# Two more blocks of a layer's second product in Strassen's form, with attention paced closer and its transposed blocks moved inside SBUF

## The chip, the cores and the metric

The kernel runs on one core of a Trainium2 chip. The metric is device time in microseconds (us) of one execution, as the median of several runs. One execution was also profiled; the rows below are of that one, and times in them count from the start of its span. The engines are TensorE (PE, with PEld for its weight loads), VectorE (DVE), ScalarE (ACT), GpSimd (POOL) and SyncE (SP), which issues nearly all DMAs.

## The reference

Inputs are float64 from NumPy, except the attention inputs (float32). What is computed, cut to what matters:

```python
# attention: batch 4, 8 heads, 768 tokens, head_dim 64, 8 memory keys; chunks of 32 tokens
q_c = q[:, :, c_start:c_end]                      # 32 tokens
k_full = concatenate([mem_k, k[:, :, l_start:r_end]])   # 16 to the left, 8 to the right
a = softmax(scale * q_c @ k_full.T); out[c] = a @ v_full
x = out as 3072 tokens x 512
# layer one, then layer two; w_in 512 x 2048, w_out 2048 x 512
h = x @ w_in;  x = maximum(0.01 * h, h) @ w_out
h = x @ w_in2; y = (h * clip(h + 3, 0, 6) / 6) @ w_out2
```

## The kernel before

**Tiling.** The 3072 tokens are six blocks of 512. Every large matmul is 128x128 by 128x512, and each product is taken three times, since operands are split in a high and a low part (`wh xh + wh xl + wl xh`). In the plain ("classical") form a block of layer one is sixteen steps f; a step is `hidden` (12 matmuls into one `ph` bank), the activation (`act_1` and `act_3` on ACT, `act_4` on DVE, which leave the split `g` in SBUF), and `output` (12 matmuls into four `py` banks that add up over f). `output` of step f-1 stands behind `hidden` of step f on TensorE. After f=15 `done` empties the four banks and `stored` writes them to `y_dram`.

In Strassen's form two blocks go together: `h_product` and `o_product` do 7 products where the plain form does 8, so 336 matmuls for each of the two products of a pair (plain: 384). The x of a pair is mixed into seven operands (`mix` L1035, `high` L1039 on ACT, `low` L1043 on DVE), as are the weights: quarters of a pair of weight tiles are summed (`c_first`, `c_more`), stored to `w_dram` (`c_store` L1007), loaded in units of 512 KB (`cw_load` L1010) and split (`cw_high` L1014, `cw_low` L1018). The activated hidden values are stored to `g_dram` (`g_store` L1089) and loaded again as operands of `o_product` (`g_load` L1092).

Before, blocks one to four of layer one are plain, blocks five and six are a Strassen pair, and all of layer two is three Strassen pairs (all hidden stages, then all output stages).

**What runs beside it.** In block one the weights of layer one arrive as float64 and are turned into float32 parts, one unit of two tiles per step: `w_load` L303, `w_upper` L313 and `w_lower` L319 on ACT, `w_clip` L323, `w_shift` L327, `w_join` L334, `w_add` L341 on DVE, `w_high` L345 on ACT, `w_low` L350 on DVE. The temporary of units 13, 14 and 15 lies in a ring `wa` of one buffer, that of the others in a ring `raw` of two. From block two on, `combine_first` (16 times) adds the parts of layer one's weights up again (`c_whole` L964), sums quarters and stores all seven; `combine` (16 times) converts a pair of tiles of layer two's weights and does the same.

Attention of tokens 1024 on goes in sixteen double visits of TensorE, `PACE` apart in the plan: scores of two pairs of chunks (L441) and the values of an earlier double visit (L617). Between them, in one buffer `both`: `a_masked_two` L475 and `a_most_two` L494 on DVE, eight exponentials L498 on ACT, `a_sums` L572 on POOL, `a_inverse` L576 on DVE, `a_norm_two` L509 (two on POOL) and a 32x32 block transpose `a_turn` L584 on DVE; then `turn_store` L587 to DRAM and three `turn_load` L590 to the layout that the values matmul reads. The values of a double visit are taken two visits after its scores.

**Order.** A planner in the kernel simulates engines, rings of buffers and a DMA pipe with the durations in `TIME`, picks at each moment the ready step with the earliest due time, and the program is written out in that order. Each engine and each DMA queue then runs its own list in order: a step that is late holds up what stands behind it. The due times of the stages come from `block_at`, `hidden_at` and `output_at`.

Of the kernel before, what the change touches and what calls it, by code (L numbers as in the profile page):

```python
# [22 lines left out]
    words=(0.67, 1.14), clip=(0.41, 0.69), shift=(0.42, 0.7), join=(0.68, 1.22), add=(0.78, 1.22), high=(0.62, 1.05), low=(0.68, 1.22), load=0.47,  # L23
# [8 lines left out]
LANDING, RATE = 2.1, 290e3  # L32
# [6 lines left out]
ORDER = (16, 18, 20, 22, 32, 34, 24, 26, 28, 30, 36, 38, 40, 42, 44, 46)  # L39
# [8 lines left out]
CLASSICAL = 4  # L48
LATEST = 0.0
W0 = 9  # L50
W1 = 0
W2 = 0
W3 = 1
W4 = 3
PACE = 17.0
LAST_STEP = 12.0
SPREAD = 3.0
# [4 lines left out]
DEEP = 1  # L62

# [125 lines left out]
def tile_kernel(  # L189
# [35 lines left out]
    CTX = LC + PT + RC  # L225
# [15 lines left out]
    turn_dram = [dr.tile([P, W // 32, 2 * HP * 32], F32, tag=f"td{j}", name=f"turn_dram{j}") for j in range(2)]  # L241
# [6 lines left out]
        [dr.tile([P, n, NF // 2, TB], F32, tag=f"gd{y}{c}", name=f"g_dram{y}{c}") for c in range(4)]  # L248
        for y, n in enumerate([(NB - CB) // 2, NB // 2])
# [8 lines left out]
    qk_t = at.tile([P, HP * (PT + W)], F32, tag="qk", name="qk_now")  # L258
    v_t = at.tile([W, HD], F32, tag="v", name="v_now")
# [92 lines left out]
    w_ready = {}  # L352

    def convert(wanted):

        for f in [0, NF, *range(1, NF)]:
# [14 lines left out]
            c = add("DVE", T["add"][n], u - 2.4, w_add, key, after=[c, l], frees=raw)  # L371
            c = add("ACT", T["high"][n], u - 1.6, w_high, key, after=[c, loaded[NPB - 1], w_ready.get((0, 0, 0))], takes=w)
# [13 lines left out]
    def inputs(pr):  # L386
        n = HP * (PT + W)
        if pr >= NPB:
            t, vt = qk_t, v_t
            if doubled(pr) and pr % 2:  # L390
                t, vt = in_t[pr][0][:, :n], in_t[pr][-1][:W, :HD]
# [8 lines left out]
    def raw_buffer(pr, j):  # L400
        in_t.setdefault(pr, []).append(raw_pair(1).rearrange("p a c -> p (a c)")[:, j * HP * (PT + W):])

    def load_qk(pr):
        if doubled(pr) and pr % 2:
            raw_buffer(pr, 0)
        nc.sync.dma_start(out=inputs(pr)[0], in_=qk[divmod(pr, PPB)])

    def load_v(pr):
        if doubled(pr) and pr % 2:
            raw_buffer(pr, 1)  # L410
        assert pr in in_t or pr >= NPB
        nc.sync.dma_start(out=inputs(pr)[3], in_=v[divmod(pr, PPB)])
# [34 lines left out]
    def a_masked(pr):  # L447
# [12 lines left out]
        for n in range(2):  # L460
            if p == 0:
                nc.vector.memset(e[n * PT:n * PT + CH, :, 0:LC], NEG)
            if p == PPB - 1:
                nc.vector.memset(e[n * PT + CH:(n + 1) * PT, :, CTX - RC:CTX], NEG)
# [7 lines left out]
    def a_masked_two(pr):  # L472
# [10 lines left out]
        for k in range(2):  # L483
            p = (pr + k) % PPB
            for n in range(2):
                if p == 0:
                    nc.vector.memset(e[n * PT:n * PT + CH, k, :, 0:LC], NEG)
                if p == PPB - 1:
                    nc.vector.memset(e[n * PT + CH:(n + 1) * PT, k, :, CTX - RC:CTX], NEG)
# [122 lines left out]
    def a_values(pr, pt, at=0, every=PT):  # L612
        t, vt = aT_t.pop(pr), inputs(pr)[3]
# [27 lines left out]
    def x_store(pr):  # L641
        at = (pr - 1) * PT - CB * TB
        nc.sync.dma_start(out=x_dram[:, :, at:at + 2 * PT], in_=out_t.pop(pr))
# [10 lines left out]
    def finish(pr, c, t, p):  # L654

        blk = pr // NPB
        if blk >= CB:
            y = [("ye", ("xs", pr))]
            c = add("ACT", T["copy"], t + 0.8, x_staged, pr, after=[c], takes=y, frees=p)
            d = add("SP", T["load"], t + 1.5, x_store, pr, after=[c], frees=y, nbytes=P * 2048)  # L660
# [30 lines left out]
    def visit_two(d, q, t):  # L691

        after, takes, frees, more, p = [], [], [], {}, None
        if d < NP:
            scores_in[d] = d
            a = add("SP", T["load"], t - 17, load_qk, d, after=loaded[-1:], takes=[("qk", d)], nbytes=P * 640 * 4)
            b = add("SP", T["load"], t - 17, load_qk, d + 1, after=[a, *scored[-1:]], nbytes=P * 640 * 4,
                    takes=[("raw", 1)] if d == 2 * NPB else [])
            loaded.extend([a, b])
            after += [a, b]  # L700
# [892 lines left out]
```

## Time and profile before

| what | value |
|---|---|
| median of 3 runs | 1051.37 us (1050.51 to 1052.44) |
| the profiled execution, its own time | 1051.67 us |
| its span, first to last instruction | 1049.9 us |
| granted TensorE clock, mean over the span | 1.000 |
| PE / DVE / ACT / POOL busy | 1037.9 / 809.0 / 612.1 / 151.2 us |
| DMA | 222.34 MB, 212 GB/s over the span |

Busy time is the time in which an engine had an instruction running. The own time is 1.8 us longer than the span, which is what lies around it. Matmuls overlap in the pipeline, so a matmul of 390 ns in a row does not cost 390 ns: rows of a chain with a count tell what one costs.

### The profile page before, as it was taken

What the parts mean: (1) busy time and instruction counts of PE and PEld (TensorE: products, weight loads), DVE (VectorE), ACT (ScalarE), POOL (GpSimd) and SP (SyncE); (2) the same over time, 40 slices, a digit from 0 to 9 for tenths busy, and PEclk for the clock granted to TensorE, in tenths of its full rate; (3) what the DMA queues carried; (4) which work ended last, traced back from release to release, by engine and by line L of the source; (5) the groups of instructions that cost most, each with busy time, mean ns of one, the idle gap of its engine ahead of it and who ended that gap; (6) DMA issues with size and microseconds to landing.
All of it is one profiled execution on the core that took longest, in us unless ns stands there. A gap on an engine that the chain in (4) does not pass through costs nothing. (4 is left out here: it accounts for less than half of the span.)

```text
span 1049.9 us, 16361 instructions
## 1 busy us (share of the span) xinstructions
PE 1037.9 (99%) x6023; PEld 851.7 (81%) x6023; DVE 809.0 (77%) x1096; ACT 612.1 (58%) x1115; POOL 151.2 (14%) x153
## 2 busy tenths in 40 slices
PE   9999999999999999999999999999999999999997
PEld 8777788888888888888888888888888888888886
DVE  6999877657676666867799997978747896686784
ACT  7886754444545555677567666657667544444451
POOL 4122111101111110012100021120365400000000
PEclk9999999999999999999999999999999999999999
DMA  9664477778777899588966865664667557257213
GB/s 291 205 210 144 155 271 240 223 240 264 235 235 249 299 273 279 184 298 286 356 223 204 266 217 186 212 233 147 227 216 255 203 150 212 51 162 193 60 56 61
DMA packets 150081, 222.34 MB, mean 212 GB/s; under 512 B 35312, under 2 KB 90608, under 8 KB 150000
## 3 DMA queue, kind: packets, MB, share of 16 engines
q1 hardware_dynamic: 148912, 221.03, 65.8%
q8 instruction: 47, 0.77, 0.3%
q10 hardware_dynamic: 1088, 0.26, 0.1%
q14 instruction: 34, 0.28, 0.1%
HBM read 137.36 MB, written 83.89 MB: 211 GB/s over the span
## 5 line engine op out<-in xcount | busy, mean ns | idle before, releaser
L836 PE MATMUL py<-g,w 128*128 128x512 f32 x768 | 188.6, 392 | 0.0
L836 PE MATMUL ph<-xh,w 128*128 128x512 f32 x512 | 171.0, 393 | 0.0
L836 PEld LDWEIGHTS py<-g,w 128*128 128x128 f32 x768 | 142.7, 188 | 29.9
L836 PEld LDWEIGHTS ph<-xh,w 128*128 128x128 f32 x512 | 95.9, 188 | 21.3 <-DVE w L350 0.8
L836 PE MATMUL ph<-xl,w 128*128 128x512 f32 x256 | 99.9, 390 | 0.6 <-DVE xl L649 0.6
L1086 POOL TENSOR_TENSOR gated<-gated,gated 128x512 f32<-128x512 f32 x32 | 51.3, 1619 | 320.0 <-DVE gated L1083 211.7
L854 ACT ACTIVATE ph<-ph 128x512 f32<-128x512 f32 x64 | 37.3, 583 | 82.4 <-PE ph L836 81.0
L1046 PE MATMUL sB<-x,cw 128*128 128x512 f32 x336 | 80.9, 389 | 0.0
L1046 PEld LDWEIGHTS sB<-x,cw 128*128 128x128 f32 x336 | 63.1, 188 | 13.1
L863 DVE TENSOR_TENSOR g<-ph,g 128x512 fp32r<-128x512 f32 x64 | 43.9, 686 | 30.9 <-ACT g L858 30.4
L1014 ACT CAST cw<-cw 128x1024 fp32r<-128x1024 f32 x56 | 58.9, 1051 | 13.4 <-DMA cw<-w_dram 13.1
L1046 PE MATMUL sE<-xwa,cw 128*128 128x512 f32 x276 | 66.4, 389 | 0.0
L1046 PE MATMUL sE<-fb,cw 128*128 128x512 f32 x264 | 63.5, 389 | 0.0
L1046 PEld LDWEIGHTS sE<-xwa,cw 128*128 128x128 f32 x276 | 51.7, 188 | 10.9 <-DVE xwa L1043 0.2
L498 ACT ACTIVATE raw<-raw,mx 128x96 f32<-128x96 f32 x128 | 46.4, 366 | 20.1 <-DVE mx L494 20.1
L1046 PEld LDWEIGHTS sE<-fb,cw 128*128 128x128 f32 x264 | 49.5, 188 | 10.5 <-DVE fb L1043 0.2
L1018 DVE TENSOR_TENSOR cw<-cw 128x1024 fp32r<-128x1024 f32 x42 | 51.6, 1235 | 6.4 <-ACT cw L1014 6.4
L836 PEld LDWEIGHTS ph<-xl,w 128*128 128x128 f32 x256 | 48.1, 188 | 10.4 <-DVE xl L649 0.9
L572 POOL TENSOR_SCALAR su<-su 128x4 f32<-128x4 f32 (+1 forms) x32 | 11.5, 360 | 265.4 <-ACT raw L498 216.4
L1046 PE MATMUL sD<-x,cw 128*128 128x512 f32 x204 | 49.3, 389 | 0.0
L1046 PE MATMUL sA<-fb,cw 128*128 128x512 f32 x204 | 49.0, 389 | 0.0
L1046 PE MATMUL sB<-xwb,cw 128*128 128x512 f32 x204 | 49.0, 389 | 0.0
(170 smaller groups left out, 2174.0 us busy)
## 6 DMA issues: line engine op xcount, KB each, us to landing
g_dram<-gated SPq DMA_DIRECT2D x128, 256.0 KB, 3.2
cw<-w_dram SPq DMA_DIRECT2D x56, 512.0 KB, 5.6
raw<-g_dram SPq DMA_DIRECT2D x32, 512.0 KB, 4.3
f<-in_moe_w_dram SPq DMA_DIRECT2D x15, 1024.0 KB, 5.0
cv<-in_moe_w_in_dram SPq DMA_DIRECT2D x8, 1024.0 KB, 6.7
w_dram<-raw SPq DMA_DIRECT2D x32, 256.0 KB, 4.3
w_dram<-cv SPq DMA_DIRECT2D x32, 256.0 KB, 2.8
cv<-in_moe_w_out_dram SPq DMA_DIRECT2D x8, 1024.0 KB, 6.7
```

The costliest lines, as they stand in the source:

```text
L498: nc.scalar.activation(out=e[:, k, :], in_=e[:, k, :], func=AF.Exp, bias=m_t[pr][:, k:k + 1], accum_out=s_t[pr][:, k:k + 1],)
L572: nc.gpsimd.tensor_scalar_add(su, su, 1e-9)
L836: nc.tensor.matmul(dst, a, b, start=first and i == 0, stop=last and i == len(terms) - 1)
L854: nc.scalar.activation(out=ph, in_=ph, func=AF.Prelu, alpha=0.01)
L863: nc.vector.tensor_sub(out=g[:, 1, :], in0=ph, in1=g[:, 0, :].bitcast(F32))
L1014: nc.scalar.copy(out=w[:, :, 0, :], in_=w[:, :, 1, :].bitcast(F32))
L1018: eng.tensor_tensor(out=w[:, :, 1, :], in0=w[:, :, 1, :].bitcast(F32), in1=w[:, :, 0, :].bitcast(F32), op=ALU.subtract)
L1046: nc.tensor.matmul(dst, a, b, start=start, stop=True, skip_group_check=True)
L1086: nc.gpsimd.tensor_tensor(out=gated(a), in0=gated(b), in1=gated(a), op=ALU.subtract)
```

## The change

- Blocks three and four of layer one (indices 2 and 3; `WHOLE = 2`) keep the plain `hidden`, but not the plain `output`. `hidden_out` activates a bank straight into a `gated` buffer, POOL takes the difference of two of them in the second block of the pair, and `g_store_two` writes two at a time to `g_dram` from ACT's queue. Their `hidden` uses the four `py` banks as a ring. In the output stage of layer one there are then two Strassen pairs, blocks three and four, and five and six.
- Three of the seven weight quarters of layer one are plain. `plain_store` writes them in block one, from the float32 temporary right behind `w_add`; that temporary is now held until these stores have landed. `combine_first` stores only the four sums, in one DMA; the other `c_store` of layer two go from four to three DMAs.
- The plan of `combine` for layer two changes from 9, 0, 0, 1, 3, 3 per stage to `WHEN = (3, 2, 2, 2, 3, 3, 1)` (there is one more stage).
- Attention: `PACE` 17.0 to 11.2, `SPREAD` 3.0 to 2.2; queries with keys, and values, of a double visit come in one load each instead of two. The memory keys stand in the middle of the window of 96, so that of the twelve 32x32 blocks of a transposed pair only eight are not zero: `turn_move` copies each of the eight inside SBUF (32 partitions x 1 KB), instead of the store and three loads through DRAM.
- `x_store` goes from SP's queue to ACT's. The order of products within stored weights (`PLACE`), the planner's `RATE`, `load` and some dependencies change.

```diff
-ORDER = (16, 18, 20, 22, 32, 34, 24, 26, 28, 30, 36, 38, 40, 42, 44, 46)
+STEP_HIDDEN = 3.5
+ORDER = (16, 18, 20, 22, 32, 34, 36, 24, 26, 28, 30, 38, 40, 42, 44, 46)
+WHOLE = 2
-W0 = 9 ... W4 = 3
-PACE = 17.0
-LAST_STEP = 12.0
-SPREAD = 3.0
+WHEN = (3, 2, 2, 2, 3, 3, 1)
+PACE = 11.2
+LAST_STEP = 10.0
+SPREAD = 2.2
...
+    def plain_store(key, n):
+        g, io = unit(key[1])[n]
+        p, e = divmod(g, 2)
+        src = tmp_t[key].bitcast(F32)[:, n, :].rearrange("p (a c) -> p a c", a=2)
+        src = src if io == e else src[:, 1:, :] if e else src[:, :1, :]
...
+        nc.sync.dma_start(out=..., in_=src)
...
             c = add("DVE", T["add"][n], u - 2.4, w_add, key, after=[c, l], frees=raw)
+            for i, (g, io) in enumerate(tiles):
+                e = add("SP", T["load"], u - 1.0, plain_store, key, i, after=[c], frees=wa, ...)
+                plain_stored.setdefault((io, g // 2), []).append(e)
             c = add("ACT", T["high"][n], u - 1.6, w_high, key, ..., takes=w)
             c = add("DVE", T["low"][n], u - 0.8, w_low, key, after=[c], frees=wa)
...
-    def turn_store(pr):
-        nc.sync.dma_start(out=turn_dram[pr // 2 % 2], in_=turned_t.rearrange("p j h c -> p j (h c)"))
-    def turn_load(pr, j):
-        nc.sync.dma_start(
-            out=aT_all[32 * j:32 * j + 32].rearrange("i r h c -> i r (h c)"),
-            in_=turn_dram[pr // 2 % 2].rearrange("(r i) j x -> i r j x", i=32)[:, :, j, :],
-        )
+    def turn_move(pr, j, r):
+        nc.sync.dma_start(out=aT_all[32 * j:32 * j + 32, r], in_=turned_t[32 * r:32 * r + 32, j])
...
+        moves = [(j, r) for r in range(P // CH) for j in (r % 2, r % 2 + 1)]
         turned_at[d + 1] = [
-            program.cell("SP", T["load"], max(t, u), turn_load, d, j, ...)
-            for j in range(W // 32)
+            program.cell("SP", T["move"], max(t, u), turn_move, d, j, r, reads=[("turned", 0)], ...,
+                         after=[w, *consumed[-1:]], nbytes=CH * 1024)
+            for n, (j, r) in enumerate(moves)
         ]
...
-            ph_t[key] = ps.tile([P, TB], F32, tag="ph", name="ph%d_%d_%d" % key, bufs=2)
+            ph_t[key] = bank("ph" if blk < WHOLE else "py", "ph%d_%d_%d" % key)
...
+    def hidden_out(blk, f, n):
+        nc.scalar.activation(out=gated(n), in_=ph_t.pop((0, blk, f)), func=AF.Prelu, alpha=0.01)
+    def g_store_two(c, s, q, n):
+        nc.scalar.dma_start(out=g_dram[0][:, c:c + 2, s, q, :], in_=fixed(f"gated{n // 2}", [P, 2, 512], "g", 2))
...
+    HIDDEN, OUTPUT = (S0, NS), ((NB - WHOLE) // 2, NS)
...
+    def hidden_kept(blk, f, t, b, ph):
+        s, n, q, h = (blk - WHOLE) // 2, blk % 2, f // 2, f % 2
+        g = count[0] % 4
+        count[0] += 1
+        cell("ACT", T["relu"], t, hidden_out, blk, f, g, writes=[("gated", g)], frees=ph, ...)
+        if h == 0:
+            return
+        g -= 1
+        if n:
+            cell("POOL", T["pool"], t + 1, g_differ, g, g + 1, reads=[("gated", g + 1)], writes=[("gated", g)])
+        e = cell("ACT", T["issue"], t + 2.5, g_store_two, 2 * n, s, q, g, reads=[("gated", g), ("gated", g + 1)], nbytes=P * 4096)
...
+        if blk >= WHOLE:
+            if key == (0, WHOLE, 0):
+                add_output(order[n - 1], t + 1, length[order[n - 1][:2]])
+            hidden_kept(blk, f, t + L, b, ph)
+            continue
```

## Rows read from the trace of the kernel before

**Rows 1.** Page, part 1: busy us (share of the span) xinstructions.
```profile
PE 1037.9 (99%) x6023; PEld 851.7 (81%) x6023; DVE 809.0 (77%) x1096; ACT 612.1 (58%) x1115; POOL 151.2 (14%) x153
```

**Rows 2.** Windows by stage: width, busy of PE, PEld, DVE, ACT, POOL; clock, DMA share, GB/s.
```profile
132.00:434.00 302.00, 302.00 (x2178) 247.88 (x2177) 206.62 (x339) 152.50 (x415) 34.52 (x48) 1.00 0.79 252
510.00:586.00 76.00, 75.97 (x335) 62.41 (x334) 67.72 (x63) 48.26 (x53) 3.11 (x2) 1.00 0.76 258
586.00:662.00 76.00, 76.00 (x336) 62.68 (x335) 69.92 (x93) 53.56 (x81) 11.16 (x6) 1.00 0.60 206
662.00:738.00 76.00, 76.00 (x337) 62.95 (x336) 66.08 (x96) 49.13 (x76) 12.10 (x8) 1.00 0.57 198
```

**Rows 3.** Waits of PE over the whole span, longest in total: us, times, longest.
```profile
PE pt L600 <- POOL e L580: 1.8, 5, 0.7
```

**Rows 4.** Chain that ended last: start us, us, what.
```profile
847.61 10.88 PE sA L1046 x48
```

**Rows 5.** Timeline of block one's end (DVE, ACT, PE): start us, us.
```profile
118.89 1.23 DVE L341 CUSTOM_DVE_ANT_0 a<-f,a 128x2048 uint16<-128x2048 uint16 x1
121.50 1.21 DVE L350 TENSOR_TENSOR w<-a,w 128x1024 fp32r<-128x1024 f32 x1
122.74 1.12 ACT L313 ACTIVATE a<-f 128x1024 f32<-128x1024 f32 x1
129.21 1.23 DVE L350 TENSOR_TENSOR w<-a,w 128x1024 fp32r<-128x1024 f32 x1 [0.51 <-ACT w L345]
131.07 0.39 PE L836 MATMUL ph<-xh,w 128*128 128x512 f32 x1
```

**Rows 6.** Stores of weight quarters, line 1007: landing; then one issue, ns min/median/max.
```profile
L1007 SPq DMA_DIRECT2D w_dram<-wa x32: 319/332/1492, 133.2 to 379.4; - x32
...
DMA to landing us min/median/max: 1.7/3.4/8.8
```

**Rows 7.** Loads through DRAM of the transposed blocks, line 590: the same.
```profile
L590 SPq DMA_DIRECT2D aT_all<-turn_dram x48: 302/424/1446, 143.2 to 400.4; - x48
...
DMA to landing us min/median/max: 2.8/3.8/6.7
```

**Rows 8.** Page, part 6: the smallest DMAs, KB each, median us to landing.
```profile
out_dram<-gated SPq DMA_DIRECT2D x4, 64.0 KB, 2.0
```

**Rows 9.** Timeline, DVE: mask and transpose, longest and shortest stay of sixteen.
```profile
195.94 1.02 DVE L475 SCALAR_TENSOR_TENSOR raw<-psc,masks 128x384 f32<-128x384 f32 x2 [1.61 <-PE psc L441]
...
208.72 0.96 DVE L584 STREAM_TRANSPOSE turned<-raw 128x768 f32<-128x768 f32 x1
...
281.03 1.01 DVE L475 SCALAR_TENSOR_TENSOR raw<-psc,masks 128x384 f32<-128x384 f32 x2
...
288.86 0.98 DVE L584 STREAM_TRANSPOSE turned<-raw 128x768 f32<-128x768 f32 x1 [0.18 <-POOL raw L509]
```

**Rows 10.** Timeline, PE: a double visit, and the hidden step behind it.
```profile
227.82 0.56 PE L441 MATMUL psc<-qk_now 64*64 64x96 f32 x16
...
229.73 0.50 PE L836 MATMUL ph<-xh,w 128*128 128x512 f32 x1
```

**Rows 11.** Groups by line and shape: count, then busy us, mean ns.
```profile
L863 DVE TENSOR_TENSOR g<-ph,g 128x512 fp32r<-128x512 f32 x64 | 43.9, 686 | 30.9 <-ACT g L858 30.4
```

**Rows 12.** Windows, instructions on tile cva alone (the combines): DVE, ACT busy.
```profile
510.00:586.00 76.00, 2.62 (x3) 1.14 (x1) 1.00 0.76 258
586.00:662.00 76.00, 8.61 (x10) 1.11 (x1) 1.00 0.60 206
662.00:738.00 76.00, 12.20 (x19) 2.28 (x2) 1.00 0.57 198
0.00:1049.00 1049.00, 95.71 (x128) 18.13 (x16) 1.00 0.66 212
```

**Rows 13.** Windows of 19 us in the output stage of layer one, columns as in rows 2.
```profile
510.00:529.00 19.00, 19.00 (x86) 15.73 (x84) 10.79 (x9) 11.19 (x13) 3.11 (x2) 1.00 0.94 345
...
548.00:567.00 19.00, 19.00 (x85) 15.73 (x85) 19.00 (x19) 14.22 (x16) 0.00 (x0) 1.00 0.61 194
```

More of the change, by code (lines that the diff above doesn't have):

```diff
@@ L62 @@
 DEEP = 1
+VALUES = 20.0
 class Program:
@@ L1160, in tile_kernel, with own, merged, gated_own @@
     swapped = add("SP", 0.0, at0 + 2 * LAST_STEP + 2, swap_pools, after=x_stored[NB - 1])
+    cell, rings_end, used, g_stored, count = program.cell, {}, {}, {}, [0]
+    def own(tag, name):
+        if name in used:
+            return dict(after=[used[name]])
+        ends = rings_end.setdefault(tag, list(program.takers.get(tag, [])))
+        used[name] = len(program.steps)
+        return dict(takes=[(tag, name)], after=ends if tag not in ("w", "wb", "x") else [])
+    def merged(*many):
+        out = {}
+        for m in many:
+            for k, v in m.items():
+                out[k] = list(out.get(k, [])) + list(v)
+        return out
+    def gated_own(n):
+        return dict(after=[swapped]) if n == 4 else own("g", f"gated{n // 2}")
+    def add_store(y, c, s, p, n, t):
+        g_stored[y, c, s, p] = cell("SP", T["load"], t, g_store, y, c, s, p, n, reads=[("gated", n)], nbytes=P * 2048)
+    def hidden_kept(blk, f, t, b, ph):
+        s, n, q, h = (blk - WHOLE) // 2, blk % 2, f // 2, f % 2
+        g = count[0] % 4
+        count[0] += 1
+        cell("ACT", T["relu"], t, hidden_out, blk, f, g, writes=[("gated", g)], frees=ph, **merged(gated_own(g), dict(after=[b])))
+        if h == 0:
[4 more added lines that the diff above has]
+        e = cell("ACT", T["issue"], t + 2.5, g_store_two, 2 * n, s, q, g, reads=[("gated", g), ("gated", g + 1)], nbytes=P * 4096)
+        g_stored[0, 2 * n, s, q] = g_stored[0, 2 * n + 1, s, q] = e
     order = [(0, blk, f) for blk in range(CB) for f in range(NF)]
@@ L1261, in tile_kernel @@
         combine_first(n % 8, n // 8, first + n * (end - first) / 16)
-    stages = [first, hidden_at[0, 0], output_at[0, 0], *(hidden_at[1, s] for s in range(NS)), output_at[1, 0] - 25]
-    for n, t, u in zip((W0, W1, W2, W3, W4, 16 - W0 - W1 - W2 - W3 - W4), stages, stages[1:]):
+    stages = [first, hidden_at[0, 0], *(output_at[0, s] for s in range(OUTPUT[0])), *(hidden_at[1, s] for s in range(NS)), output_at[1, 0] - 25]
+    assert sum(WHEN) == 16
+    for n, t, u in zip(WHEN, stages, stages[1:]):
         combine_between(n, t, u)
-    rings_end = {r: list(program.takers.get(r, [])) for r in rings}
-    used = {}
-    def own(tag, name):
-        if name in used:
-            return dict(after=[used[name]])
-        used[name] = len(program.steps)
-        return dict(takes=[(tag, name)], after=rings_end[tag] if tag not in ("w", "wb", "x") else [])
-    def merged(*many):
-        out = {}
-        for m in many:
-            for k, v in m.items():
-                out[k] = list(out.get(k, [])) + list(v)
-        return out
     def wide_own(y, c):
@@ L1448, in load @@
                     if dst[0] == "x":
+                        before = list(program.takers["x"])
                         more = own("x", f"o{dst[2]}{w // 2}_{y}")
+                        if "takes" in more:
+                            more["after"] = before
                     taken["x"] = cell("SP", T["load"], due, g_load, y, c, s, w, dst, writes=[dst], nbytes=P * 4096,
@@ L1512, in tile_kernel @@
         for u in range(4, UNITS):
-            add_weights(y, 0, u, wanted(y, u) - 4, "DVE")
-        for s in range((S0, NS)[y]):
+            add_weights(y, 0, u, wanted(y, 0, u) - 4, "DVE")
+        for s in range(HIDDEN[y]):
             if s:
@@ L1518, in tile_kernel @@
                 add_hidden(y, s, (2 * g, 2 * g + 1), hidden_at[y, s] + 2 * g * PROD * H6)
-        for u in range(UNITS):
-            add_weights(y, 1, u, output_at[y, 0] + u * 4 * H6 - 20, "POOL" if y else "DVE")
-        for s in range((S0, NS)[y]):
+        for u in sorted(range(UNITS), key=lambda u: wanted(y, 1, u)):
+            add_weights(y, 1, u, wanted(y, 1, u) - 20, "POOL" if y else "DVE")
+        for s in range(OUTPUT[y]):
             add_outputs(y, s)
```

220 lines of the change are left out of this document (115 added, 105 removed).

## Prediction

> **What bounds the kernel now.** I read the page first: TensorE is busy 1037.9 of 1049.9 us [rows 1]. A busy PE need not be a full one, so I went to the waits of PE: the longest in total is 1.8 us over the whole span [rows 3], and between 132 and 738 us PE has no idle time to speak of in any stage [rows 2]. So in these stages a matmul taken away is time gained, as long as nothing else turns late. The chain that ended last then gives the price: 48 large matmuls in a row take 10.88 us, 226.7 ns each [rows 4] (the 390 ns of a single one overlap). Last I looked at what could turn late. DVE is the only other engine near its limit: in the output stage of layer one it is busy 19.00 of 19 us [rows 13], while PE does not wait, so the order in which DVE takes its work already saves PE there. At the end of block one PE follows the conversion of weights [rows 5]. DMA is at 0.94 of its share and 345 GB/s in one window of 19 us [rows 13], and between 0.57 and 0.79 over whole stages [rows 2].
>
> **The change part by part.**
>
> *TensorE.* Blocks three and four lose 2 x 192 plain output matmuls and get one Strassen output of 336. That is 48 fewer of 226.7 ns: **-10.88 us** [rows 4]. Hidden products, attention's matmuls and layer two are the same in number. A double visit of PE is 1.9 us [rows 10] wherever it stands.
>
> *Plain stores in block one.* Units 13, 14 and 15 share one temporary buffer. In the rows, unit 14's add ends at 120.12, its low part at 122.71, and unit 15's first conversion starts at 122.74: the buffer is what unit 15 waited for, and the low part comes 2.59 us behind the add [rows 5]. Now the buffer is also held by two stores issued behind the add. Two issues are about 0.33 us apart, and a store of quarters lands after 3.4 us in the median [rows 6]: 0.33 + 3.4 = 3.7 us, but DMA is quiet there, so I take 3.4 in all. Each link of the chain grows by 3.4 - 2.6 = 0.8 us. There are three: unit 13's load waits for a temporary of the same kind held by unit 11, and then 13 to 14 and 14 to 15. That makes 2.4 us. The low part of unit 15 ended at 130.44 and its hidden matmuls started at 131.07 [rows 5], so 0.6 us is free: **+1.8 us**. Bounds: with the shortest landing, 1.7 us, the stores are done before the low part and it costs nothing; with a landing of 4.3 us (0.9 above the median of rows 6) it is 3 x 2.0 - 0.6 = 5.4.
>
> *Attention closer together.* One double visit must now fit in 11.2 us. Its buffer `both` is held from the mask to the end of the block transpose: the shortest of sixteen stays is 281.03 to 289.84 = 8.8 us, the longest 195.94 to 209.68 = 13.7 [rows 9]; the middle of these two, 11.3, is about the new pace. The long ones come of loose due times, which the change tightens. Values are taken two visits, 22.4 us, after the scores, so a stay that is 2.5 us too long can be made good in the next. I take 0; the upper bound is the next item's.
>
> *Moves.* Eight `turn_move` replace a store and three loads. They may start only when the visit before has read the layout buffer, and the next visit's values wait for the last of them. The loop is a visit 1.9 [rows 10], eight issues of 0.42 = 3.4 and one landing. No row shows a DMA inside SBUF: the nearest in path is the load of the transposed blocks, 2.8 to 6.7 us, median 3.8 [rows 7], the nearest in size the 64 KB store with 2.0 [rows 8]. With 2.0 the loop is 7.3 us, with 3.8 it is 9.1, with 6.7 it is 12.0. I take 3.8, as the moves sit in the same queue and the same traffic as those loads: 2.1 us under the pace, so **0**. What hides it is the plain and hidden matmuls between two visits. The queue of SP issues them: what stands behind a move that waits is quarters and weight units wanted much later.
>
> *Conversions of layer two, moved.* A `combine` is 95.71 / 16 = 6.0 us of DVE [rows 12]. The first stage has six fewer. From 132 to 434 DVE was busy 206.6 us [rows 2]; now 6 x 6.0 = 36 go, and 32 low parts of `g` at 0.686 = 22 [rows 11]: about 149 us. The stretch shrinks from 302 to some 213 us (planned: 16 steps of 6.3, 32 of 3.5): 70% against 68%. Tight are the last output stage of layer one and the first two hidden stages of layer two. They showed 67.7, 69.9 and 66.1 us of DVE in 76 each [rows 2], of which combines were 2.6, 8.6 and 12.2 [rows 12]. With 2, 3 and 3 combines in their place the stages come to 77.1, 79.3 and 71.9: the first two want 4.4 us more than they have, and the third has 4.1 left. Conversions are wanted last, and 19.00 of 19 us on DVE did not make PE wait [rows 13]. I take 0, with 4.4 us as the upper bound.
>
> *The rest at nothing.* Between blocks two and three the new hidden banks need one of the four sums to be emptied; two output matmul groups of 1.36 us cover a copy of some 0.7 us; up to 0.7 us if they don't. `hidden_out` has four banks and so three steps of 2.7 us (12 x 226.7 ns) to be late in. The stores on ACT's queue stand in front of exponentials; a wait for POOL there goes to the stay in `both`, above.
>
> *Sum.* 1051.67 (profiled execution) - 10.88 + 1.8 = 1042.6; the median of the runs is 0.3 lower than that execution, so **1042.5 us**.
>
> **A rule that speaks against it.** The turned blocks went through DRAM in pieces of 128 KB that landed after 3.8 us [rows 7]. The Trainium skill, DMA: Bandwidth & Descriptors, section Bandwidth, says to batch DMAs to at least 1 MiB, and that transfers under 64 KB are dominated by their fixed cost, which its section on the anatomy of one DMA puts at about 2.0 us. Eight moves of 32 KB, paid one by one, would by that page be an estimated 8 x 2.1 = 16.6 us, over the pace by more than 5 us in each of fourteen visits, and the time would be above 1110 us; in flight together they would be 3.4 + 2.1, less than I took. The trace agrees with the fixed part, 2.0 us for 64 KB [rows 8], and shows the three loads issued 0.42 us apart with landings of 3.8 us [rows 7], thus in flight together; I follow the row; the page's case is the slower rival below, in whose chance it is counted.
>
> **The rivals.**
>
> *Clean.* The plain stores land before the low part, so block one is unchanged: 1051.4 - 10.9 = 1040.5. For it: shortest landing 1.7 us [rows 6]. Against it: the median of 3.4. If a small wait of before goes as well [rows 3], 1039.5.
>
> *VectorE becomes the bound* where two output stages and three combines follow each other: the 4.4 us above reach PE, 1046.9. For it: DVE without a gap for tens of us [rows 13]. Against it: PE did not wait then.
>
> *Slower: the loop of moves.* If the landing is as the longest of rows 7, the loop is 12.0 us plus a wait of SP of 0.4 for a step in front; 1.2 us over the pace in fourteen visits is 17 us: 1059. It decides from (1051.4 - 1042.5) / 14 = 0.64 us over the pace, a landing of some 6.5 us. For it: traffic is denser: 252 GB/s over 302 us [rows 2] are 76 MB, of which some 33 go (six combines 12, blocks three and four's sums 2, the way through DRAM 13, plain stores 6; the combines' figures from 1 MB loaded and 0.9 stored each) and some 13 come (8.4 of `g`, 4.2 of moves), so about 56 MB in 213 us, 264 GB/s, and each move has SP's queue to go through. Against it: the median of rows 7.
>
> *Doesn't pay.* Waits in several of these places together eat the 10.88 us, PE is no longer the bound from block two to four, and the time stays near 1051.
>
> **How the numbers follow.** Forecast (1041 to 1046) 0.46; clean 0.16; VectorE 0.16; doesn't pay 0.08; slower 0.14. A measurement of this kernel can tell some 0.2%, 2.1 us, from no change. The first three cases are faster: 0.78; same 0.08; slower 0.14. The range goes from the clean case, 1039.5, to the edge of the case that doesn't pay, 1051.0, and leaves out the slower one and part of that.
>
> **What would show it.** Right: about 5975 PE instructions, no wait of PE for `aT_all` (moves) between 130 and 330 us, hidden products of blocks five and six starting some 90 us earlier, one or two new waits of PE for `w` near 125 to 135 us. Wrong: waits of PE's values matmul (L617's successor) for a DMA into `aT_all`; PE waiting for DVE's low parts in the second output stage; landings of moves above 6 us; a block one longer by more than 5 us.

## The result and the profile after

The changed kernel takes **1058.7 us** (median of 4 runs, 1056.0 to 1059.9) against 1051.1 for the kernel before beside it: ratio 1.0062, 95% interval 1.0050 to 1.0074. It is slower, and the prediction of 1042.5 (1039.5 to 1051.0) is wrong. The profiled execution took 1058.72 us, its span 1056.9.

The work that should go did go. The page's first part, which answers to [rows 1], and a row of the chain that ended last, which answers to [rows 4]:

```profile
PE 1034.4 (98%) x5978; PEld 846.5 (80%) x5978; DVE 834.2 (79%) x1108; ACT 624.9 (59%) x1115; POOL 166.5 (16%) x161
```

```profile
843.69 10.88 PE sE L1063 x48
```

A large matmul still costs 226.7 ns, and the trace holds 4176 of them for 4224: 48 fewer, 10.88 us. So 6.9 + 10.9 = 17.8 us were lost elsewhere (the last matmul starts at 1050.4 us for 1043.5). The starts of the stages, read from TensorE's records, say where:

```
                                      before    after    lost, less the 226.7 ns of each large matmul taken out
first hidden product                    29.9     32.3    2.4
  to the hidden products of the pair   402.5    324.2    8.7   (384 matmuls, 87.0 us, less)
hidden products of the pair             76.2     81.6    5.4
its output (after: two outputs)         76.6    153.6    0.8   (336 matmuls, 76.2 us, more)
layer two, to its last matmul          458.3    458.8    0.5
```

Of the 8.7 us, 1.8 lie in block one (109.8 us for 108.0) and 6.9 in blocks two to four.

The waits of PE, longest in total, name the places (us in total, times, longest); before, the largest was 1.8 [rows 3]:

```profile
PE px L633 <- DMA aT_all<-turned: 4.4, 2, 2.3
PE sB L1063 <- ACT gated L1093: 2.8, 2, 2.6
PE py L853 <- DVE g L880: 1.3, 2, 1.2
PE px L633 <- ACT aT_all L625: 1.3, 1, 1.3
```

The clock adds to them. Windows around three of these waits, columns as in [rows 2]; before, the clock was 1.00 in every stage of [rows 2] and 1.000 as the mean over the span:

```profile
33.00:43.00 10.00, 9.28 (x62) 7.03 (x63) 9.85 (x14) 9.13 (x19) 2.85 (x3) 0.83 0.75 238
...
320.00:330.00 10.00, 5.57 (x45) 4.43 (x44) 3.44 (x7) 4.42 (x19) 4.85 (x5) 0.84 0.80 236
...
410.00:430.00 20.00, 17.36 (x70) 13.88 (x69) 13.05 (x16) 14.52 (x22) 3.07 (x2) 0.91 0.92 307
```

Behind each wait TensorE ran for a while at the lower level, 1.2 GHz (the half clock, below): 10 x 0.17 + 10 x 0.16 + 20 x 0.09 = 5.1 us in all. That is more than a quarter of the 17.8.

**The moves.** Line 609 is `turn_move` (issue in ns min/median/max, then landing). [Rows 7] had 302/424/1446 and 2.8/3.8/6.7 for the loads that it replaces:

```profile
L609 SPq DMA_DIRECT2D aT_all<-turned x128: 507/584/1747, 145.7 to 332.9; - x128
...
DMA to landing us min/median/max: 1.7/2.9/7.3
```

To 285 us the eight moves of a set take 5 to 6 us of SP's queue, and once, at 215 us, 7.9, 2.5 of them in the wait that is explained below. Then come these three sets (timeline of SP, with what stands ahead of the third), and the visit that waits for the last of them (timeline of PE):

```profile
287.55 9.73 SPq L609 DMA_DIRECT2D aT_all<-turned  x8
...
302.34 8.47 SPq L609 DMA_DIRECT2D aT_all<-turned  x8
...
312.04 2.31 SPq L1024 DMA_DIRECT2D w_dram<-cva  x2
314.46 1.25 SPq L1024 DMA_DIRECT2D w_dram<-cv  x1
315.80 0.57 SPq L434 DMA_DIRECT2D qv_now<-in_v_dram  x1
316.47 7.82 SPq L609 DMA_DIRECT2D aT_all<-turned  x8
```

```profile
324.07 0.30 PE L633 MATMUL px<-aT_all,raw 96*64 96x64 f32 x2 [2.17 <-DMA aT_all<-turned]
326.64 1.79 PE L633 MATMUL px<-aT_all,raw 96*64 96x64 f32 x30 [2.27 <-DMA aT_all<-turned]
```

No single issue takes that long; SP stands still between them. Of its waits from 285 to 330 us, 20.3 us in all, 10.1 are put down to transfers that have nothing to do with the moves, the largest of them:

```profile
SPq L609 <- DMA w_dram<-raw: 2.3, 1, 2.3
SPq L609 <- DMA raw<-in_qk_dram: 2.3, 2, 1.2
...
SPq L609 <- DMA x_dram<-xs: 1.8, 2, 1.4
```

The trace's records say why. All 703 transfers of this kernel, from SP's and ACT's queues together, carry one of eight semaphores, nearly in turn, and each waits until the former transfer on its own has landed. The set at 316 us:

```
move issued   semaphore   former transfer on it         that one landed
318.33        106         cwS load, issued 311.54       318.32
320.28        108         w_dram store, 312.04          320.26
321.84        101         w_dram store, 314.46          321.82
322.80        103         values load, 315.80           322.78
323.78        104         x_dram store, 318.40          323.77
```

So at most eight transfers are in flight (the most that the records show at any time is eight), a set of moves needs all eight places, and a place in this table comes free when a transfer of 256 to 512 KB has landed, 5 to 8 us after its issue. Summed over SP's queue this wait is some 10 us between 288 and 330 us, and 0.0 in the kernel before from 30 to 345. The kernel's source names no semaphore: whether the eight belong to the chip or to the way in which the program is built, no run here shows.

The places are not all of it for the set at 316 us. The visit before it ended at 313.52, and most sets are issued 0.04 us behind their visit; this one came 2.95 us behind, since a `combine`'s stores and a load stood ahead of it in SP's list. From first issue to last landing it then took 9.9 us, where sets without a wait for places take 6.2 to 7.3.

**The head.** The first temporary is held by its plain store. ScalarE's timeline and the same store in the chain that ended last:

```profile
28.83 1.12 ACT L310 ACTIVATE a<-f 128x1024 f32<-128x1024 f32 x1 [0.77 <-DMA w_dram<-a]
29.85 0.57 ACT L625 COPY aT_all<-pt 96x512 f32<-96x512 f32 x1
```

```profile
21.39 7.33 DMA w_dram<-a
```

The store was 7.33 us in flight; ScalarE's next conversion waits 0.77 us for it, the attention's copy (L625) stands behind that in ScalarE's list, and TensorE waits 1.3 us for the copy.

**The hidden pair.** ScalarE's timeline. The weight load (`cwS`) lands late. Behind its high part on ScalarE stand the copies (L1086), behind its low part on VectorE the sum (L1090), the rectify (L1093) needs both, and TensorE waits 2.6 us for the rectify:

```profile
415.08 1.05 ACT L1031 CAST cwS<-cwS 128x1024 fp32r<-128x1024 f32 x1 [1.55 <-DMA cwS<-w_dram]
416.04 1.06 ACT L1086 COPY small_ye<-sB 128x512 f32<-128x512 f32 x2
418.03 1.20 ACT L1093 ACTIVATE gated<-sB 128x512 f32<-128x512 f32 x2 [0.93 <-DVE sB L1090]
```

### The profile page after: what moved, and what is told of

It reads as the page before. It is cut to its first block, busy times and chain, and to the rows that moved or that the text cites. A ratio compares the mean times of both kernels' runs of the same rounds, so it can differ in the third digit from the quotient of the medians.

```text
span 1056.9 us, 16413 instructions
## 1 busy us (share of the span) xinstructions
PE 1034.4 (98%) x5978; PEld 846.5 (80%) x5978; DVE 834.2 (79%) x1108; ACT 624.9 (59%) x1115; POOL 166.5 (16%) x161
## 4 chain that ended last, share of the span: by engine, by line
PE 73%; DVE 10%; DMA 9%; ACT 3%; issue 3%; SPq 0%; POOL 0%; DVEq 0%; ACTq 0%; POOLq 0%
PE sA L1063 18%; PE sE L1063 16%; PE sB L1063 15%; PE ph L853 10%; PE sD L1063 7%; PE py L853 4%; PE px L633 2%; DMA cwL<-w_dram 1%; PE psc L463 1%; DMA cwS<-w_dram 1%; DMA x_dram<-xs 1%; DMA w_dram<-a 1%; DMA f<-in_moe_w_dram 1%; DMA g_dram<-gated 1%; DMA cv<-in_moe_w_in_dram 1%
## 5 line engine op out<-in xcount | busy, mean ns | idle before, releaser
L853 PE MATMUL py<-g,w 128*128 128x512 f32 x384 | 96.6, 396 | 1.3 <-DVE g L880 1.3
L853 PEld LDWEIGHTS py<-g,w 128*128 128x128 f32 x384 | 70.4, 188 | 17.0 <-DVE g L880 2.2
L1063 PE MATMUL sB<-x,cwL 128*128 128x512 f32 x288 | 69.8, 389 | 0.0
L1063 PEld LDWEIGHTS sB<-x,cwL 128*128 128x128 f32 x288 | 54.0, 188 | 11.4 <-DVE gated L1100 0.2
L1063 PE MATMUL sE<-xwa,cwL 128*128 128x512 f32 x240 | 58.1, 390 | 0.7 <-DVE xwa L1060 0.7
L1063 PE MATMUL sE<-fb,cwL 128*128 128x512 f32 x240 | 58.1, 390 | 0.0
L853 PEld LDWEIGHTS ph<-xl,w 128*128 128x128 f32 x256 | 48.8, 191 | 10.2 <-DVE xl L665 0.5
L1063 PEld LDWEIGHTS sE<-xwa,cwL 128*128 128x128 f32 x240 | 44.9, 188 | 10.7 <-DVE xwa L1060 1.2
L1063 PEld LDWEIGHTS sE<-fb,cwL 128*128 128x128 f32 x240 | 45.0, 188 | 9.7 <-DVE fb L1060 0.4
L1063 PE MATMUL sB<-xwb,cwL 128*128 128x512 f32 x192 | 46.1, 389 | 0.0
L1086 ACT COPY small_ye<-sB 128x512 f32<-128x512 f32 x64 | 36.8, 591 | 14.8 <-PE sB L1063 14.7
L1063 PE MATMUL sD<-x,cwL 128*128 128x512 f32 x156 | 37.6, 389 | 0.0
```

The lines of the kernel that those rows point to most:

```text
L853: nc.tensor.matmul(dst, a, b, start=first and i == 0, stop=last and i == len(terms) - 1)
L1063: nc.tensor.matmul(dst, a, b, start=start, stop=True, skip_group_check=True)
L1086: nc.scalar.copy(out=small(n), in_=sums(letter, k))
```

## Experiments

**Theory:** the 10.9 us are real; what is late is late through transfers, at three places (head, last moves, hidden pair), each with a half clock behind it. **Rivals:** the moves are the wrong way altogether; VectorE or the pace of the attention is the bound; a wait that is taken away only uncovers the next. Each run has its time, and its ratio to the kernel before beside it (95% interval).

**1. Head spared**. The plain stores of the first three units are left out, and their pairs of quarters stored later.

```diff
-            for i, (g, io) in enumerate(tiles):
+            for i, (g, io) in enumerate(tiles) if f not in (0, 16, 1) else ():
```

> The first three weight units (those at the head of block one) are not stored plain there; their two pairs of quarters are stored later, from the sums, as in the kernel before. All else is the changed kernel. Theory (a store holds the temporary that ScalarE's next step needs, ScalarE's queue holds the attention's copy, TensorE waits, and the clock halves behind that wait): the first hidden product starts near 30 us instead of 32.3, no half clock at 33 us, and the whole is 2.4 + 1.7 = 4.1 us shorter, about 1054.6. Rival (a head that starts earlier only waits longer at the next thing that is late): first hidden product near 30 but the whole within 1.5 us of 1058.7.

1059.6 us, 1.0075 (1.0055 to 1.0096): the rival. The first hidden product starts at 30.5 us, and TensorE then waits for the attention's next pair, whose row stands first among its waits:

```profile
PE pt L617 <- POOL e L603: 4.4, 4, 2.0
```

The half clock comes behind one of these waits, at 35.7 us. The store is what the head waits for; there is another chain just behind it.

**2. Through DRAM again**. One `turn_store` and three `turn_load` as in the kernel before, in place of the moves.

> The turned weights of the attention's pairs go through DRAM again, by one store and three loads in place of eight moves in SBUF; all else is the changed kernel. Theory (a move costs more to issue than I took and the last ones land late, but eight of them are still the shorter way): a store of some 3 us and loads of 3.8 us behind it put every visit later, so TensorE waits at the end of the attention, 7 to 13 us over the changed kernel, 1066 to 1072. Rival (the moves are what the change loses by): the two waits for the turned weights at 321 and 324 us go, with the half clock behind them, and it is about 6 us shorter, 1052.

1063.8 us, 1.0115 (1.0101 to 1.0128). The rival "the moves are what it loses by" falls, and the theory missed too, in the time (1066 to 1072) and in the place. The waits for the turned weights are gone, but the first Strassen products wait for their operands, 13 us in seven kinds of waits between 340 and 485 us; the two largest:

```profile
PE sA L1070 <- ACT x L1063: 4.4, 1, 4.4
PE sA L1070 <- DVE x L1067: 2.9, 1, 2.9
```

**3. Two queues**. `(nc.scalar if r % 2 else nc.sync).dma_start(...)` for the moves.

> Of the eight moves of each pair four are issued by ScalarE's queue and four by SyncE's; all else is the changed kernel. Theory (the issue of 0.58 us each on one queue, up to 1.7, is what makes the last pairs late): a pair's moves take about 3.5 us in place of 5 to 6, the waits of 2.3 and 2.3 us for them and the half clock behind go, 1052.5. Rival (the landing under a DMA share of 0.86 is what is late, or ScalarE's other steps are held up by issues): the waits stay, 1057 or more.

1063.5 us, 1.0106 (1.0093 to 1.0119): as its rival has it (1057 or more). ScalarE's transfers share the eight places with SP's, so half of the moves now wait in ScalarE's list, in front of exponentials and rectifies (ScalarE's waits, 220 to 345 us):

```profile
ACT raw L520 <- DMA aT_all<-turned: 18.0, 3, 6.5
ACT gated L1103 <- DMA aT_all<-turned: 13.0, 4, 4.3
```

**4. No combine in the hidden pair**.

```diff
-WHEN = (3, 2, 2, 2, 3, 3, 1)
+WHEN = (3, 0, 3, 3, 3, 3, 1)
```

> No weight pair of layer two is combined in the hidden products of the pair (0 for 2), three for two in the first output stage and in the second; all else is the changed kernel. Theory (a combine there takes the DMA queue and 6 us of VectorE, so a weight load lands late and ScalarE holds the rectify behind it): the wait of 2.8 us at 415 us goes with the half clock at 419, 4.5 us shorter, about 1054. Rival (the output stages have no more room either): the waits move to 440 to 590 us, within 1.5 us of 1058.7.

**1053.65 us**, 1.0022 (1.0011 to 1.0033): as the theory has it. The stage takes 76.3 us for 81.6, with no idle time of PE and the full clock (windows of this run; then the first of them in the changed kernel, whose second stands above):

```profile
356.00:410.00 54.00, 54.00 (x239) 44.52 (x238) 46.99 (x56) 41.79 (x65) 8.16 (x5) 1.00 0.93 307
410.00:430.00 20.00, 20.00 (x90) 16.54 (x89) 13.81 (x17) 16.84 (x26) 3.43 (x2) 1.00 0.88 307
...
356.00:410.00 54.00, 53.69 (x236) 43.78 (x236) 43.53 (x51) 38.60 (x60) 9.27 (x5) 1.00 0.85 283
```

The DMA share (the mean busy share of the 16 DMA engines) is no lower over the stage, 0.91 for 0.86 from 356 to 438 us. So it was not the traffic as a whole, but the two combines that stood among the steps that TensorE needed next. Whether by their transfers or by their 6 us of VectorE each, this run does not separate. The first output stage, which has one combine more, takes 1.4 us longer (78.8 for 77.4).

**5. All plain stores later**. Everything that `plain_store` does goes back to `combine_first`.

> No quarter of layer one's weights is stored plain in block one; all are stored later, from the sums, as in the kernel before. All else is the changed kernel. Theory (the plain stores cost only the head, 2.4 us and the half clock of 1.7 us behind it, and give back more at the end of the attention, where the stores would otherwise stand in front of the weights' loads): first hidden product near 30 us with no half clock at 33 us, block one near 108 us, but a new wait of TensorE between 345 and 365 us of some 6 us for late weights, 1059 to 1063 in all. Rival (the plain stores are the loss): 1052 to 1055, with no new wait.

1061.5 us, 1.0091 (1.0078 to 1.0104). As expected at the far end: block one 108.3 us, and two waits of 1.7 and 3.6 us near 368 us for late operands: as a whole the plain stores earn more than they cost. The head is not settled by it: an input load was late at 14 us, and the first hidden product started at 33.5.

**6. Two combines beside the attention**. `WHEN = (2, 0, 4, 3, 3, 3, 1)`: run 4 with the combine that stood at 312 us moved as well.

> The fourth run's kernel (no combine in the hidden pair) with one more combine moved: two for three beside the attention, four for three in the first output stage. Theory (the third combine's stores on SyncE's queue, at 312 to 316 us, and its load are what puts the last moves late): the two waits for moves near 320 us go with the half clock behind them, 4.5 to 6 us under that run's 1053.65, so 1048 to 1049, under the kernel before. Rival (the moves are slow by themselves beside the weights' loads, at a DMA share of 0.86): the waits stay and the output stage gets more of VectorE, 1053 to 1056.

1057.05 us, 1.0056 (1.0044 to 1.0068): **the theory as I had it falls.** The combine's stores in front of the moves were not the cause alone: the late set starts 0.46 us behind its visit for run 4's 2.75, but it is 13.1 us from there to its last landing for run 4's 10.2. The last two late sets took 9.5 and 10.7 us of SP's queue, and TensorE's wait is as long as ever:

```profile
PE px L633 <- DMA aT_all<-turned: 4.9, 2, 3.6
```

What took its place as a theory is the eight places, as read from the records above.

**7. Matmuls in the wait**. 72 small matmuls in run 4's late visit.

> The fourth run's kernel with 72 small matmuls of a tile of zeros put into the visit that waits for moves near 320 us, 36 ahead of its products and 36 behind the first two, where the two waits are; their result is used nowhere. Theory (the wait's end is set by the moves, and the half clock comes of TensorE's idleness in it): the two waits are filled, the visit ends when it did, and the 3.4 us at half clock behind it go, 1.0 to 1.7 us under 1053.65, so 1052 to 1052.7. Rival (the half clock does not hang on that wait): it stays near 327 us and the time is 1053.5 or more.

1058.1 us, 1.0068 (1.0052 to 1.0083): inconclusive. The 72 took 5.7 us, and a wait of 2.3 us stood behind them all the same, with a half clock of 3.4 us; whether the clock can be held in this way was not shown.

**8. The moves in the kernel before**. At its pace of 17 us, with the window's order that lets eight do.

> The kernel before with the moves in SBUF alone (eight a pair, with the reordered window that lets eight do) in place of one store and three loads through DRAM; pace 17 us, everything else as before. Theory (the moves' price is only paid where the pace leaves no room): each pair's moves are through in 6 to 10 us of the 17 and TensorE waits for none, within 3 us of the kernel before, 1049 to 1055. Rival (eight issues a pair on SyncE's queue put the weights' loads late wherever they stand): 1056 to 1062.

1054.4 us, 1.0030 (1.0018 to 1.0042): at the edge of what I gave the theory. TensorE waits for no move; by stages the 2.7 us to its last matmul are 1.4 in the Strassen stages of layer one, 1.1 in the head, 1.1 beside the attention and 0.4 in layer two, less 1.3 in block one. What a move is without a crowd:

```profile
L586 SPq DMA_DIRECT2D aT_all<-turned x128: 507/588/1337, 139.8 to 405.0; - x128
...
DMA to landing us min/median/max: 1.8/1.9/4.0
```

1.9 us for 32 KB agrees with the about 2.0 us that the Trainium skill, DMA: Bandwidth & Descriptors, gives in the anatomy of one DMA; the page has it for a transfer that GpSimd issues, and these are SyncE's.

**9 and 11. No moves at all.** Eight transposes of 32 partitions write each block where it belongs, into two buffers in turn; run 11 has the pace at 12.0.

```diff
+        for j in (r % 2, r % 2 + 1):
+            nc.vector.transpose(out=t[32 * j:32 * j + 32, r], in_=both(pr)[32 * r:32 * r + 32, :, 32 * j:32 * j + 32])
```

> The fourth run's kernel (no combine in the hidden pair, 1053.65) without any moves: eight transposes of 32 partitions a pair write each block of the turned weights straight to its place, in two buffers that alternate, in place of one transpose of 128 partitions and eight transfers. VectorE gets some 1.5 us more a pair. Theory (every transfer waits until the transfer eight places ahead of it has landed, since all carry one of eight semaphores in turn; eight moves a pair fill all eight, and between 288 and 330 us they stand 10.7 us in that wait): both waits of TensorE near 320 us and the half clock behind them go, no transfer waits for the eighth before it between 248 and 355 us, 4.5 to 6 us less, 1047.6 to 1049. Rival (the transfers' bytes, not their number, fill the time to 330 us): loads of queries, keys and values then land late and TensorE waits for those, 1052 to 1055.

> The kernel without moves (eight transposes in place, no combine in the hidden pair) with the attention's pace at 12.0 us for 11.2. Theory: as without moves at pace 11.2, with fewer waits in block two since VectorE's additional 1.5 us a pair has more room, 1046 to 1049, under the kernel before by 0.2% or more. Rival (the attention now ends too late for the hidden pair): a new wait of TensorE of over 3 us between 345 and 365 us, 1050 to 1053.

1075.1 us, 1.0229 (1.0213 to 1.0244), and 1069.1, 1.0165 (1.0151 to 1.0179): misses by 26 and 20. Near 320 us no transfer waits for a place any more, but block two, where VectorE also splits `g` and sums quarters, takes 121.4 us in run 9 for 104.2 in run 4. TensorE's two longest waits of run 9:

```profile
PE ph L840 <- DVE g L867: 4.9, 2, 4.3
PE ph L840 <- DVE xl L662: 3.9, 2, 3.7
```

A transpose of 32 partitions takes 0.43 us, so a pair 3.5 for 0.98, and VectorE's list holds `g` behind it. The Trainium skill, Vector Engine (DVE) Microarchitecture Reference, section 3.8, calls moves across quadrants of 32 partitions free for an instruction of at most 32 partitions: the traces agree for one instruction, 422 to 443 ns in runs 9 and 11 whichever quadrant it writes. But eight of them stand here for one.

**10. The moves on GpSimd's queue**, with run 4's `WHEN`, and **13. the same, with each engine's order as in run 4**: `nc.gpsimd.dma_start` for the moves.

> The fourth run's kernel with all eight moves of a pair issued by GpSimd, in place of SyncE; nothing else differs. Theory (the eight semaphores in turn are what makes the moves late): if GpSimd's transfers carry others, the moves stand in no wait for the eighth transfer before, and SyncE's own transfers stand 0 to 3 us in it between 248 and 355 us; TensorE's waits for the moves go unless GpSimd issues a move slower than in 1 us, 1048 to 1052. Rival (SyncE's queue is late for its bytes): its waits stay, 1053 and more.

> The fourth run's kernel (1053.65), each engine's order kept, with the moves issued by GpSimd's queue instead of SyncE's. Theory of places: the moves of the last pairs start together when the earlier visit is done and TensorE's waits near 320 us fall from 4.5 us to under 2, with no new wait in the hidden pair since its order is the fourth run's, 1050 to 1052. Theory of bytes: the moves land 5 to 8 us after issue as in the other run on that queue, the waits stay at 4 us or more, 1053 to 1057.

1062.35 us, 1.0104 (1.0090 to 1.0117), and 1058.7, 1.0060 (1.0046 to 1.0073; the profiled execution of run 13 took 1054.6). GpSimd's transfers do carry eight semaphores of their own, and SP's wait for places is 0.0 us from 142 to 330 us in both runs; in run 4 it was some 10 from 288 to 330. TensorE's wait for the set near 320 us falls from 4.5 us to 1.6 in run 13, and to as much in run 10, as the theory of places has it, but no time comes of it. In run 13 a wait of 3.3 us follows one visit later, at 336 us:

```profile
PE px L633 <- DMA aT_all<-turned: 5.5, 3, 3.3
```

In run 10, whose order was planned anew, the hidden pair takes 85.0 us for run 4's 76.3. And the moves, sent without a wait, land later. Not only in the crowd: from 145 to 250 us, at a DMA share of 0.62 in run 4 and 0.64 in run 13, the landings are, of run 4 and then of run 13:

```profile
DMA to landing us min/median/max: 1.8/2.7/5.4
...
DMA to landing us min/median/max: 2.0/4.5/6.2
```

From 288 to 330 us a transfer of run 10 takes 6.4 us in the mean for 4.5 in run 4, with 7.3 in flight for 5.6 and a DMA share of 0.91 for 0.86; in run 13 it is 5.6 us, with 6.7 in flight and a share of only 0.82. The places are what the moves visibly wait for in run 4. Whether a nearly full DMA stands behind them these two runs do not show, since they also change the queue, and on this one a move lands late at a low share too.

**12. No combine beside the attention**. `WHEN = (0, 0, 4, 4, 4, 3, 1)`.

> No weight pair of layer two is combined beside the attention nor in the hidden pair (0 and 0), four in each output stage and the first hidden stage of layer two; all else is the changed kernel. It takes some 5.5 MB of transfers out of the time from 142 to 356 us and puts them later, where they cost waits of their own. Theory of bytes: TensorE's waits for moves near 320 us shrink under 1 us in all, and so does the time that transfers stand behind the eighth before them from 288 to 330 us (10 us to under 4). Theory of places (eight in flight at most, filled by the moves themselves): both stay, 4 us and some 10 us. The whole says nothing here, since layer two gets the work: 1055 to 1062 either way.

1067.3 us, 1.0148 (1.0129 to 1.0168); the whole says nothing, as stated. The wait for moves is between the two theories, and so is SP's wait for places, some 7.5 us for 10:

```profile
PE px L633 <- DMA aT_all<-turned: 2.7, 2, 1.8
```

**14. The last six pairs in place**. Run 4, with the transposes of run 9 for pairs 10 to 15 alone, where only hidden products run beside them.

> The fourth run's kernel with the last six pairs turned in place by eight transposes of 32 partitions on VectorE (0.43 us each, 3.5 us a pair) and without moves; the first ten pairs keep their moves. Theory (only the moves of the last pairs are late, by places or by bytes, and beside the hidden products alone VectorE has the room that it had not in block two): TensorE's waits for turned weights near 320 us go with the half clock, block two as in the fourth run, 1047.5 to 1049.5, under the kernel before. Rival (the chain of one pair from visit to visit has no slack at this pace, and VectorE's 2.5 us more put it over): waits of TensorE for the turned weights, now from VectorE, of 3 us or more stay, 1052 to 1056.

**1050.9 us**, 0.9998 (0.9986 to 1.0009): 2.75 us under run 4 and level with the kernel before. The waits are as the theory has it, the time is 1.4 us above its range. Blocks three and four, beside which the attention ends, take 104.0 us for 108.8, PE is busy and the clock full there (288 to 330 us; in run 4 PE was busy 37.5 us of the 42, and the mean clock 0.96), and its wait for turned weights is 0.7 us:

```profile
288.00:330.00 42.00, 41.92 (x328) 33.90 (x322) 38.17 (x75) 21.89 (x68) 12.49 (x13) 1.00 0.86 271
```

```profile
PE px L647 <- ACT aT_all L639: 2.1, 1, 2.1
...
PE px L647 <- DVE aT_all L616: 0.7, 1, 0.7
```

The first row is the head, where the first hidden product starts at 34.0 us here for 31.6 in run 4: again a plain store, 7.97 us in flight, in front of ScalarE's conversion.

**15. With the head of the kernel before**. Run 14, with run 1's spared stores and the planner's prices of the kernel before: its 290 GB/s for the first 130 us, and its 0.47 us for an issue on SP throughout, not only there.

> The last run's kernel (no combine in the hidden pair, the last six pairs turned in place, 1050.9) with the head of the kernel before: the first three weight units are not stored plain in block one but later, and the order of the first 130 us is planned with the kernel before's price of a transfer (290 GB/s and 0.47 us an issue). Theory (a store that is 7 to 8 us in flight holds the temporary that ScalarE's next step needs, and with it the first hidden product): first hidden product at 30 to 31 us for 34.0, no chain through a plain store there, no half clock near 35 us, 3 to 5 us less, 1046 to 1048, under the kernel before. Rival (another chain of the head, the attention's own, ends as late): first hidden product at 32 us or later or block one longer by as much, 1049.5 to 1052.

**1049.2 us**, 0.9983 (0.9972 to 0.9994): under the kernel before by 0.17%, between the theory (1046 to 1048) and the rival. First hidden product at 31.2 us, no half clock (same window as in the changed kernel, which had 0.83), no store in the chain there:

```profile
33.00:43.00 10.00, 9.54 (x71) 7.04 (x70) 9.23 (x15) 10.00 (x21) 1.28 (x3) 1.00 0.61 204
```

Its last matmul starts at 1040.9 us for 1043.5. Of the 10.9 us, 2.6 come through; the other 8.3 are still spread thin: 1.2 in the head, 4.5 in blocks one to four, 0.7 in the Strassen stages of layer one, 1.8 in layer two, with no single wait over 1.8 us from 30 us on.

## Why the prediction was wrong

- **TensorE, -10.88: right.** 48 matmuls of 226.7 ns are gone, and run 15 shows a part of it in the time. What failed is the terms that were put at nothing, or had none: the 17.8 us are 2.4 in the head, 1.8 in block one, 6.9 in blocks two to four (6.1 of them the wait for moves and its half clock), 5.4 in the hidden pair and 1.3 behind it.
- **Moves, "I take 0": the step that failed.** The loop of 9.1 us (1.9 + 3.4 + 3.8) was about the right size where transfers are few: in run 8 fourteen of sixteen sets take 6.2 to 7.5 us from first issue to last landing, 8.1 to 9.4 with the visit, with 0.59 us an issue for my 0.42 and a shorter landing. But from first issue to last landing the three late sets took 11.7, 9.8 and 9.9 us (from the records), so with a visit of 1.9 the loop was 13.6, 11.7 and 11.8 against a pace of 11.2: 3.5 us over in all, and TensorE waited 4.4. I priced a move by its issue and its landing; what sets the late ones is the eighth transfer before them, and for the last also what stands ahead of it in SP's list (2.95 us). My slower rival had this place and even this time, 1059, but the time by luck: it wanted 1.2 us in fourteen visits, and it was one visit, with losses elsewhere. "Landings of moves above 6 us", which I named as a sign, were there (7.3), and so was TensorE's wait for a DMA into `aT_all`.
- **Plain stores, +1.8 at block one's end: the right wait in the wrong place.** The last unit's first conversion does wait for a store there, 3.23 us, and TensorE 0.5 for it. What cost was the head, for which I had no term: a store lands there after 7.3 us, where I had taken 3.4 for block one's end, and the half clock comes behind: 2.4 + 1.7 us. That block one itself is longer by just the 1.8 us of the forecast is luck, since 1.7 of them are that half clock. Runs 14 and 15 agree with this chain, and run 1 shows that another stands close behind it.
- **Conversions, 0 with 4.4 as a bound: right where I looked, wrong where I did not.** The output stages and layer two lost 1.3 us in all. The 5.4 us were lost in the hidden pair, the stage that I had not summed, and not to VectorE's sum over a stage but to a late weight load and what stands behind it on ScalarE and VectorE; run 4 gives them back.
- **The clock was in no term.** Waits of 1.3, 4.4 and 2.6 us drew 5.1 us of half clock behind them. In kind, "doesn't pay", 1051 from several small waits, was the nearest case, and the clock is most of what it lacked.
- **The Trainium skill's rule on small transfers** (DMA: Bandwidth & Descriptors, Bandwidth) was weighed with two readings, an estimated 16.6 us for eight moves paid one by one or 3.4 + 2.1 in flight together. The traces agree with the second to 285 us, where most sets take 6.2 to 7.3 us; behind that neither held, 9.8 to 11.7 us, since no more than eight transfers of any size were in flight.

Open stays how much of the late moves belongs to the eight places and how much to the fullness of the DMA: runs 10 and 13 took the first away, but onto a queue where a move lands late anyway, and run 12 eased the second and both shrank. Run 14 takes the late moves themselves away and leaves the question.

## What to carry to other kernels

Count transfers, not only bytes: where each waits for an earlier one on the same semaphore, a burst of small ones waits for the large ones that are in flight, and stands in front of everything else on its queue. When a schedule is tightened, sum each stage that gets closer, the head and the transitions too, with landings from the busy time and not from the median, and allow for a half clock behind TensorE's waits (here 1.7 us behind each of three). And a gain on the busiest engine is worth only as much slack as the chains beside it have: here three changes (runs 4, 14 and 15) were needed before 1.9 of the 10.9 us showed.

## What the runs showed of the hardware

- In this program the transfers of SP's and ACT's queues together carry eight semaphores and those of GpSimd's eight more (runs 10 and 13), and no more than eight of either were in flight at a time. A wait for the former transfer on the same one is shown as a wait for an unrelated tile.
- A transfer of 32 KB between partitions of SBUF costs SP's queue 0.58 us and lands after 1.9 us in the median (run 8), 2.9 in the changed kernel. GpSimd issues one in 0.50 us, and it lands after 5.4 (run 10) and 4.8 (run 13).
- Behind waits of 1.3 to 4.4 us TensorE was often granted 1.2 GHz for 3.4 us, sometimes for 6.8 and in run 2 for 10.2, and lost half of that; in the kernel before, with no wait over 0.7 us once it had started, never until its last matmul. It is no fixed rule: the head of the changed kernel fell behind a wait of 1.3 us, while waits of 1.3 to 1.8 us in the Strassen stages of runs 4, 8 and 15, one of 1.6 us in run 9's head and one of 2.0 us in run 1's hidden pair drew none.
